# A residual attention and mixer layer on one core: another order of all operations, and the residual sums shared between VectorE and GpSimd

## The chip, the core and the metric

The kernel runs on one core of a Trainium2 chip. Its engines work side by side, each through its own list of instructions, and wait for each other by semaphores: TensorE (PE, matmuls; its weight loads are shown as PEld), VectorE (DVE), ScalarE (ACT), GpSimd (POOL) and SyncE (SP), which issues DMA transfers only. The metric is the device time of one execution in microseconds (us).

## The reference, cut to what matters

The input is one sequence of 2048 rows of 448 values in bf16. The layer normalises it, runs a sliding-window attention, adds the result to the input, and does the same once more with a mixer and MLP. The kernel must give `h2`.

```python
def _A_ref(x, wqkv, wo):                      # 16 heads of 28
    q, k, v = heads(x @ wqkv)
    idx = pos[:, None] - 2 * arange(8)[None, :]          # 8 keys, every second row back
    logits = einsum("bhsd,bhswd->bhsw", q, k[idx]) * 28 ** -0.5   # masked where idx < 0
    return merge(einsum("bhsw,bhswd->bhsd", softmax(logits), v[idx])) @ wo

def _B_ref(x, w1, w2, w3, w4):
    h = gelu(layernorm(x) @ w1)
    hs = shifted(h) @ w2          # four quarters of h, shifted by 1, -1, 2, -2 rows
    x1 = x + hs
    return x1 + gelu(layernorm(x1) @ w3) @ w4

h  = x + _A_ref(layernorm(x), A_wqkv, A_wo)
h2 = h + _B_ref(layernorm(h), B_w1, B_w2, B_w3, B_w4)
```

So the output is the sum of `h`, of `x1` (which holds a normalised `h`), and of the MLP's result.

## The kernel before, in words

**Tiles and phases.** The 2048 rows are 16 tiles of 128 rows, in four strips of four tiles. All of the sequence stays on the chip. For each strip the attention runs through these phases: N1 (statistics and normalising of x), A1 (projection to q and k, kept transposed), V (projection to v), A2 (products of q with the eight shifted k on VectorE, tile `qk_r`, which TensorE adds up per head), S (softmax: tiles `mx`, `ls`, `pb`), A3 (VectorE spreads the probabilities over a band with a mask, tile `bd_r` out of `bmask`, and TensorE multiplies the band with v, tile `vw`), O (projection by wo and addition of x). Then, per strip, B1 (layer norm, w1 and a gelu into the transposed hidden state). The second half runs over five units of tiles, 0-1, 2-5, 6-9, 10-13 and 14-15: B2 (w2 and the residual, `x1` in f32), T (layer norm of `x1`, a transposition), W3 (w3 and gelu, tile `h3T`) and B3 (w4 and the store, tile `ost`).

**Halos.** The attention looks 14 rows back, so a strip needs the end of the strip before it. Four small on-chip copies per strip bring it there, issued by SP; their sources are written by ScalarE's copies out of PSUM. In the order listings they are `arena<-arena` of 64x4x16, 64x3x16, 64x16 and 128x3x16.

**The residual sums.** After the layer norm of `x1` has read a tile, `phase_B2` adds `xin` (the tile `h`) to it: `xb[i] += xin[i]`, 128 x 448 in f32, once for each of 16 tiles (lines 919 and 920, shown as `arena<-arena,xin`). `store` (line 943) needs that sum, and the small product `mrs`, minus the mean times the reciprocal deviation, 128 x 4, which `rstd` (line 547) makes once per strip: it is the part of the normalised `h` that is the same for a whole row.

**What sets the order.** The program isn't emitted as it is written. Each operation is first recorded, with its engine and what it reads and writes (`_Sched.add` and `group`, lines 144 and 147); there are 858. `arrange` (line 194) then takes a table of numbers, `ORDER`: it is the sequence of all operations, and so the order on each engine, in SP's list of transfers, and the order in which the buffers of a pool are handed out (eight PSUM banks, three `lntm` of the layer norm, four `actT`, three `bd_r`, five `ost`, sixteen `h3T`). A second table, `OTHER`, names operations that take their alternative engine; until now only copies and normalises have one (ScalarE or VectorE, `copy`, line 403, and `normalize`, line 551). `_emit_plan` (line 247) sets the semaphores, and `emit_engine` (line 1002) writes the instructions, which is why all of them have line L1011 in the profile. `block` is an attribute of an operation that the recording keeps; nothing in `arrange` or `_emit_plan` reads it.

Of the kernel before, what the change touches and what calls it, by code (L numbers as in the profile page):

```python
# [6 lines left out]
ALU = mybir.AluOpType  # L7
# [12 lines left out]
STAGE = '....'  # L20
ALONE = False
ORDER = """
# [29 lines left out]
"""  # L52
OTHER = """
91 94 114 187 188 501 507 549 550
"""
FULL = (4,)
FILL = (1, 1, 0, 0)
# [228 lines left out]
def bass_sequential_preLN__sliding_local_dilated__mixer_s_mlp__prompt_kernel(  # L286
# [16 lines left out]
    S = _Sched()  # L303
# [16 lines left out]
    with ExitStack() as es:  # L320
        def sb(name, shape, dt):
            return es.enter_context(nc.sbuf_tensor(name, shape, dt))
        AR = sb("arena", [128, A_END], BF16)
        xin = sb("xin", [128, NTL, D], BF16)
# [17 lines left out]
        rs_y = sb("rs_y", [128, 3, 2, NTL], F32)  # L342
        mrs = sb("mrs", [128, NTL], F32)
        nm = sb("nm", [128, 3, NTL], F32)
# [21 lines left out]
        def arv(off, parts, n):  # L366
            return AR[0:parts, off:off + n]
# [12 lines left out]
        xb = [arv(A_KV + i // 4 * KVB, 128, 4 * D * 2).bitcast(F32).rearrange("p (i d) -> p i d", d=D)[:, i % 4, :] for i in range(NTL)]  # L380
# [18 lines left out]
        def act(out_ap, in_ap, func, **kw):  # L399
            table = {ACT.Exp: "exp", ACT.Ln: "exp", ACT.Gelu_apprx_tanh: "gelu"}.get(func)  # L400
            return S.add("act", "activation", table=table, out=out_ap, in_=in_ap, func=func, **kw)
# [7 lines left out]
        def dve(meth, block=False, **kw):  # L409
            op = S.add("dve", meth, **kw)  # L410
            op.block = block
            return op

        def pool(meth, **kw):
            return S.add("pool", meth, **kw)
# [90 lines left out]
        def rstd(kind, i, m=4, summed=False, norms="v", how="p"):  # L506
            var = mv[:, kind, i:i + m, 1]
            by = 1.0 / D if summed else 1.0
            first = int(kind == 1)
            shifted_ = "a" in norms  # L510

            def power(k):
                S.add("pool", "tensor_tensor", out=rs_y[:, kind, k, i:i + m], in0=rs_x[:, kind, k, i:i + m], in1=mhalf[:, 0:m], op=ALU.pow)

            def power_act(k):
                act(rs_x[:, kind, k, i:i + m], var, ACT.Ln, scale=by * (1.0 + EPS * k), bias=epsilon[:, k:k + 1])
                act(rs_y[:, kind, k, i:i + m], rs_x[:, kind, k, i:i + m], ACT.Exp, scale=-0.5)

            def shift(k):
                if m == 1:  # L520
                    act(nmr[:, kind, i:i + 1], nm[:, kind, i:i + 1], ACT.Identity, scale=rs_y[:, kind, k, i:i + 1])
                else:
                    dve("tensor_tensor", out=nmr[:, kind, i:i + m], in0=nm[:, kind, i:i + m], in1=rs_y[:, kind, k, i:i + m], op=ALU.mult)

            if not summed and (shifted_ or kind == 1):
                dve("tensor_scalar", out=nm[:, kind, i:i + m], in0=mv[:, kind, i:i + m, 0], scalar1=-1.0, scalar2=None, op0=ALU.mult)
            if how == "a":
                power_act(first)
                if shifted_:
                    shift(first)  # L530
                if kind == 1:
                    power_act(0)
            else:
                if kind == 1:
                    dve("tensor_scalar", out=rs_x[:, kind, 1, i:i + m], in0=var, scalar1=by * (1.0 + EPS), scalar2=EPS * EPS, op0=ALU.mult, op1=ALU.add)
                    power(1)
                    if shifted_:
                        shift(1)
                if kind == 1 or summed:
                    dve("tensor_scalar", out=rs_x[:, kind, 0, i:i + m], in0=var, scalar1=by, scalar2=EPS, op0=ALU.mult, op1=ALU.add)  # L540
                else:
                    dve("tensor_scalar", out=rs_x[:, kind, 0, i:i + m], in0=var, scalar1=EPS, scalar2=None, op0=ALU.add)
                power(0)
                if kind != 1 and shifted_:
                    shift(0)
            if kind == 1:
                pool("tensor_tensor", out=mrs[:, i:i + m], in0=nm[:, 1, i:i + m], in1=rs_y[:, 1, 0, i:i + m], op=ALU.mult)

        CHUNK = (0, 128, 192, 320)

# [337 lines left out]
        def phase_B2(u):  # L888
# [28 lines left out]
            for n, i in enumerate(tiles):  # L917
                normalize(2, i, ln, n, xb[i], TURN["B2"][u], summed, norms[n])
            for i in tiles:
                S.add("pool", "tensor_tensor", out=xb[i], in0=xb[i], in1=xin[:, i, :], op=ALU.add).block = True  # L920
            b2_a[u] = transposed(ln, TURN["B2"][u], len(tiles))

        h3 = {}
# [129 lines left out]
```

## Time and profile before

| what | value |
| --- | --- |
| time, median of 3 runs | 191.43 us (191.26 to 191.53) |
| profiled execution, its own time | 191.99 us |
| span of that execution in the trace | 190.3 us |
| PE busy | 180.0 us (95%), 2434 matmuls |
| DVE busy | 129.9 us (68%) |
| ACT busy | 123.4 us (65%) |
| POOL busy | 26.5 us (14%) |
| 16 residual sums on GpSimd | 17.1 us, 1086 ns each |
| granted TensorE clock | 1.00 |

In the rows of the profile an operation is named by engine, line, operation and `out<-in`, with buffer numbers left out; `xN` counts instructions that were put together. The bracket at a row's end is the idle time of the engine ahead of it and what ended that. A DMA row's time ends with its landing where the row says so, and SPq is the queue of SP's issues.

### The profile page before, as it was taken

To read this page: it belongs to the slowest core of one execution; us is meant where nothing else is said; L and a number is where in the kernel's file an instruction comes from. 1 tells how busy PE (TensorE), PEld (TensorE's weight loads), DVE (VectorE), ACT (ScalarE), POOL (GpSimd) and SP (SyncE) were. 2 spreads that over 40 slices of the span, in tenths; PEclk is the share of its full clock that TensorE was granted. 3 is DMA by queue.
4 is the path that set the end of the run, shared out by engine and by line. 5 is a ranking of instruction groups with operands and counts; after the bars stand their busy time and mean duration, and the time that the engine had idled before them with its cause. 6 is when DMAs were issued, how large, how long until landed. Compare 5 with 4: busy or idle time off the path is not lost.

```text
span 190.3 us, 5623 instructions
## 1 busy us (share of the span) xinstructions
PE 180.0 (95%) x2434; PEld 96.3 (51%) x2434; DVE 129.9 (68%) x226; ACT 123.4 (65%) x282; POOL 26.5 (14%) x61
## 2 busy tenths in 40 slices
PE   6699999897999989999989999999999999999994
PEld 2496433354443545565645535545444454455672
DVE  6999999999999999998998940099850006002203
ACT  3459999998999999999644897910256303650250
POOL 2250000000010000002205100181386002000000
DMA  5950254477407895796250060015044004000031
GB/s 147 339 193 3 44 110 110 78 174 158 103 3 114 160 272 225 136 331 134 50 113 0 5 134 0 3 30 108 0 91 119 0 0 112 19 3 0 17 109 48
DMA packets 36577, 18.06 MB, mean 95 GB/s; under 512 B 25304, under 2 KB 36040, under 8 KB 36552
## 3 DMA queue, kind: packets, MB, share of 16 engines
q1 hardware_dynamic: 36552, 17.70, 38.3%
q8 instruction: 19, 0.31, 0.7%
q14 instruction: 6, 0.05, 0.1%
HBM read 7.91 MB, written 1.84 MB: 51 GB/s over the span
## 4 chain that ended last, share of the span: by engine, by line
PE 56%; DVE 22%; ACT 11%; DMA 5%; SPq 2%; issue 2%; DVEq 0%; ACTq 0%
PE ps L1011 56%; DVE qk_r L1011 6%; DVE lntm L1011 5%; DVE bd_r L1011 4%; DMA arena<-in_A_wqkv_dram 3%; ACT lntm L1011 3%; SPq L1011 2%; DMA wo_s<-in_A_wo_dram 2%; ACT arena L1011 2%; DVE arena L1011 1%; ACT xin L1011 1%; DVE mx L1011 1%; DVE st L1011 1%; ACT h3T L1011 1%; ACT rs_x L1011 1%
## 5 line engine op out<-in xcount | busy, mean ns | idle before, releaser
L1011 PE MATMUL ps<-actT,arena 64*128 64x512 bf16 (+1 forms) x756 | 69.4, 329 | 0.9 <-ACT h3T L1011 0.4
L1011 ACT ACTIVATE h3T<-ps 128x512 bf16<-128x512 f32 (+1 forms) x70 | 30.8, 518 | 41.2 <-PE ps L1011 41.0
L1011 PEld LDWEIGHTS ps<-actT,arena 64*128 64x128 bf16 x756 | 37.3, 94 | 28.5 <-PE ps L1011 2.1
L1011 PE MATMUL ps<-arena,h3T 64*128 64x448 bf16 (+2 forms) x434 | 44.9, 343 | 0.4 <-DVE arena L1011 0.3
L1011 DVE SCALAR_TENSOR_TENSOR ost<-ps,mrs,arena 128x448 bf16<-128x448 f32 (+1 forms) x17 | 10.8, 650 | 40.6 <-PE ps L1011 40.6
L1011 ACT ACTIVATE arena<-ps 128x512 bf16<-128x512 f32 (+3 forms) x63 | 31.5, 541 | 3.7 <-PE ps L1011 3.2
L1011 PEld LDWEIGHTS ps<-arena,h3T 64*128 64x128 bf16 (+1 forms) x434 | 22.9, 94 | 20.0 <-DVE arena L1011 0.7
L1011 DVE TENSOR_TENSOR qk_r<-arena 128x4096 bf16<-128x4096 bf16 (+1 forms) x16 | 32.0, 2013 | 0.3 <-PE ps L1011 0.3
L1011 DVE TENSOR_TENSOR bd_r<-arena,bmask 80x2048 bf16<-80x2048 bf16 x16 | 19.8, 1270 | 0.1
L1011 POOL TENSOR_TENSOR arena<-arena,xin 128x448 f32<-128x448 f32 x16 | 17.1, 1086 | 14.8 <-DVE lntm L1011 14.8
L1011 DVE TENSOR_SCALAR lntm<-arena,mv,rs_y 128x512 bf16<-128x512 f32 x14 | 8.9, 679 | 12.2 <-ACT rs_y L1011 11.7
L1011 PE MATMUL ps<-wo_s,actT 64*128 64x448 bf16 x128 | 14.8, 350 | 1.1 <-DMA wo_s<-in_A_wo_dram 1.0
L1011 PE MATMUL ps<-w_s,arena 64*128 64x448 bf16 (+1 forms) x128 | 14.2, 350 | 0.1
L1011 PE MATMUL ps<-actT,w_s 64*112 64x512 bf16 x112 | 13.4, 378 | 0.0
L1011 ACT ACTIVATE actT<-ps 128x512 bf16<-128x512 f32 (+2 forms) x18 | 11.2, 653 | 3.2 <-PE ps L1011 3.2
L1011 PE MATMUL ps<-arena,actT 64*128 64x448 bf16 x112 | 13.2, 350 | 0.1
L1011 ACT ACTIVATE lntm<-xin,nm 128x448 bf16<-128x448 bf16 x16 | 10.5, 662 | 3.6 <-DVE nm L1011 3.6
L1011 POOL TENSOR_TENSOR mrs<-nm,rs_y 128x4 f32<-128x4 f32 x4 | 1.5, 387 | 71.9 <-ACT rs_y L1011 70.1
L1011 DVE SCALAR_TENSOR_TENSOR arena<-xin,rs_y,ps 128x448 f32<-128x448 bf16 x16 | 10.4, 667 | 0.0
L1011 DVE BATCH_NORM_STATS2 st<-xin 128x6 f32<-128x448 bf16 x16 | 9.2, 611 | 0.9 <-DMA xin<-in_A_x_dram 0.9
L1011 PEld LDWEIGHTS ps<-wo_s,actT 64*128 64x128 bf16 x128 | 5.6, 94 | 7.6 <-PE ps L1011 1.5
L1011 PEld LDWEIGHTS ps<-actT,w_s 64*112 64x112 bf16 x112 | 7.0, 127 | 4.7 <-DMA actT<-lntm 0.4
(70 smaller groups left out, 158.0 us busy)
## 6 DMA issues: line engine op xcount, KB each, us to landing
arena<-in_B_w_dram SPq DMA_DIRECT2D x2, 896.0 KB, 6.5
out_dram<-ost SPq DMA_DIRECT2D x15, 112.0 KB, 2.0
arena<-in_B_w_dram SPq DMA_DIRECT2D x2, 784.0 KB, 5.7
vw<-vt SPq DMA_DIRECT2D x4, 320.0 KB, 3.8
vw<-vt SPq DMA_DIRECT2D x4, 256.0 KB, 3.6
arena<-in_A_wqkv_dram SPq DMA_DIRECT2D x2, 448.0 KB, 4.7
xin<-in_A_x_dram SPq DMA_DIRECT2D x2, 448.0 KB, 7.2
xin<-in_A_x_dram SPq DMA_DIRECT2D x3, 224.0 KB, 5.9
```

The source lines that it names most:

```text
L1011: inst = getattr(eng, meth)(**kw)
```

## The change

Three things change.

1. `mrs` is made by VectorE instead of GpSimd: four products of 128 x 4.
2. A residual sum may be made by GpSimd or by VectorE. Operations 685, 686, 755, 756, 815, 816 and 551 take VectorE, so seven of the sixteen sums stand there and nine stay on GpSimd. The attribute `block` of the sums goes.
3. `ORDER` is another sequence of the same 858 operations. In `OTHER` the copies 91, 114, 501 and 507 and the normalise 188 leave, so ScalarE does them; the normalise 189 enters.

VectorE's operations go from 216 to 223, ScalarE's from 244 to 248, GpSimd's from 57 to 46; TensorE's 262 groups (2434 matmuls) and SP's 79 transfers are the same.

```diff
 ORDER = """
-29 0 6 7 1 2 30 31 8 48 49 50 51 9 53 54 52 11 10 60 61 58 59 32 55 56 57 62 63 64 65 39 40 41 42 43 44 45 46 47 87 89
...
+29 0 1 6 7 33 34 35 5 8 48 9 53 49 39 40 41 42 43 44 45 46 47 30 32 2 50 54 11 10 58 51 52 60 59 55 61 56 62 57 63 65
...
 OTHER = """
-91 94 114 187 188 501 507 549 550
+94 187 189 549 550 551 685 686 755 756 815 816
 """
...
             if kind == 1:
-                pool("tensor_tensor", out=mrs[:, i:i + m], in0=nm[:, 1, i:i + m], in1=rs_y[:, 1, 0, i:i + m], op=ALU.mult)
+                dve("tensor_tensor", out=mrs[:, i:i + m], in0=nm[:, 1, i:i + m], in1=rs_y[:, 1, 0, i:i + m], op=ALU.mult)
...
             for i in tiles:
-                S.add("pool", "tensor_tensor", out=xb[i], in0=xb[i], in1=xin[:, i, :], op=ALU.add).block = True
+                both = dict(out=xb[i], in0=xb[i], in1=xin[:, i, :], op=ALU.add)
+                S.add("pool", "tensor_tensor", alts=[("dve", [("tensor_tensor", both)])], **both)
```

The first place is VectorE at the end of the attention, where the last strip's softmax (`mx`, `pb`) and band products (`bd_r`) meet the first unit's layer norm (`st`, `mv`, `lntm<-arena`). Before:

```order
L1011 TENSOR_SCALAR rs_x<-mv 128x4
L1011 TENSOR_REDUCE mx<-ls 128x64
L1011 TENSOR_TENSOR pb<-ls,mx 128x8x64
L1011 TENSOR_SCALAR lntm<-arena,mv,rs_y 128x512 x2
L1011 TENSOR_SCALAR nm<-mv 128x4
L1011 TENSOR_SCALAR lntm<-arena,mv,rs_y 128x512
L1011 TENSOR_TENSOR bd_r<-arena,bmask 80x2048 x2
L1011 TENSOR_SCALAR lntm<-arena,mv,rs_y 128x512
L1011 TENSOR_TENSOR bd_r<-arena,bmask 80x2048
L1011 CAST actT<-ps 128x512
L1011 TENSOR_TENSOR bd_r<-arena,bmask 80x2048
L1011 CAST actT<-ps 128x512
```

and after:

```order
L1012 TENSOR_REDUCE mx<-ls 128x64
L1012 BN_STATS st<-arena 128x6
L1012 BN_AGGR mv<-st 128x2
L1012 TENSOR_TENSOR arena<-arena,xin 128x448
L1012 BN_STATS st<-arena 128x6
L1012 TENSOR_TENSOR mrs<-nm,rs_y 128x4
L1012 TENSOR_SCALAR nm<-mv 128x4
L1012 BN_AGGR mv<-st 128x2 x3
L1012 TENSOR_SCALAR rs_x<-mv 128x4
L1012 TENSOR_TENSOR pb<-ls,mx 128x8x64
L1012 TENSOR_SCALAR lntm<-arena,mv,rs_y 128x512
L1012 TENSOR_TENSOR bd_r<-arena,bmask 80x2048 x3
```

Behind these rows follow three normalises, the last product and then B3's eviction; the two casts are ScalarE's now, a residual sum and `mrs` have come in, and `pb` stands behind the statistics.

The second place is GpSimd from the end of the attention on, with `mrs`, the residual sums and the powers of the layer norm. Before:

```order
L1011 TENSOR_TENSOR rs_y<-rs_x,mhalf 128x4
L1011 MEMSET arena 128x4x2
L1011 TENSOR_TENSOR mrs<-nm,rs_y 128x4
L1011 TENSOR_TENSOR arena<-arena,xin 128x448
L1011 TENSOR_TENSOR mrs<-nm,rs_y 128x4
L1011 TENSOR_TENSOR arena<-arena,xin 128x448 x3
L1011 TENSOR_TENSOR mrs<-nm,rs_y 128x4
L1011 TENSOR_TENSOR arena<-arena,xin 128x448 x4
L1011 TENSOR_TENSOR rs_y<-rs_x,mhalf 128x2
L1011 TENSOR_TENSOR rs_y<-rs_x,mhalf 128x4
L1011 TENSOR_TENSOR arena<-arena,xin 128x448 x8
```

and after:

```order
L1012 TENSOR_TENSOR arena<-arena,xin 128x448
L1012 MEMSET mhalf 128x8
L1012 TENSOR_TENSOR rs_y<-rs_x,mhalf 128x4
L1012 TENSOR_TENSOR arena<-arena,xin 128x448
L1012 MEMSET arena 128x4x2
L1012 TENSOR_TENSOR arena<-arena,xin 128x448 x5
L1012 TENSOR_TENSOR rs_y<-rs_x,mhalf 128x4
L1012 TENSOR_TENSOR arena<-arena,xin 128x448 x2
L1012 TENSOR_TENSOR rs_y<-rs_x,mhalf 128x2
```

The products are gone, nine sums are left of sixteen, and most of them stand between the two powers.

The third place is SP's list after the loads of wqkv, with the halos of the first strips. Before:

```order
L1011 DMA xin<-in_A_x_dram 128x4x448 x2
L1011 DMA arena<-arena 128x3x16
L1011 DMA arena<-arena 64x4x16
L1011 DMA arena<-arena 64x3x16
L1011 DMA arena<-arena 64x16
L1011 DMA_TRANSPOSE actT<-lntm 128x16x128
L1011 DMA vw<-vt 16x3x512
L1011 DMA arena<-arena 64x3x16
```

and after:

```order
L1012 DMA xin<-in_A_x_dram 128x4x448
L1012 DMA arena<-arena 128x3x16
L1012 DMA xin<-in_A_x_dram 128x4x448
L1012 DMA vw<-vt 16x512
L1012 DMA arena<-arena 64x4x16 x2
L1012 DMA arena<-arena 64x16
L1012 DMA arena<-arena 64x3x16 x2
L1012 DMA_TRANSPOSE actT<-lntm 128x16x128
```

The 64x4x16 of the second strip and the 64x16 now stand ahead of the first 64x3x16. A little further on in the same list stood one load of wo, a 128x3x16 and three loads of wo; now there are two loads of wo, a 64x16, a load, a 64x3x16 and the last load.

56 rows, old and new, of the table ORDER are left out of this document.

## The prediction

> **What bounds the kernel now.** I read the chain of work that ended last first, because it says whose time counts where; then the busy time by stretches cut where the chain changes hands; then the timelines of the engines around each place where the chain leaves TensorE. These are four of the chain's 151 pieces, with start, length, engine and what it works on.
>
> ```profile
> 8.52 13.31 PE ps L1011 x209
> 39.90 4.17 DMA wo_s<-in_A_wo_dram
> 67.47 10.59 PE ps L1011 x164
> 127.75 59.27 PE ps L1011 x623
> ```
>
> The last piece is to be noted: from 127.75 us to 187.0 the chain is TensorE without a break. Ahead of it the chain changes hands often (VectorE, ScalarE, a load of wo), so an edit can win or lose time there, and from 127.75 on only if it makes TensorE wait. The stretches show the same. Columns are the stretch, its length, busy us and instructions of each engine, the granted clock, the share of the DMA engines, GB/s.
>
> ```profile
> core 0: us, PE busy (x) PEld busy (x) DVE busy (x) ACT busy (x) POOL busy (x), PEclk, DMA share, GB/s
> 8.50:97.30 88.80, 84.99 (x1435) 46.18 (x1435) 86.72 (x135) 80.53 (x192) 7.02 (x31) 1.00 0.55 133
> 97.30:127.75 30.45, 29.75 (x345) 15.39 (x346) 17.41 (x37) 19.99 (x39) 7.14 (x9) 1.00 0.20 40
> 127.75:187.70 59.95, 59.93 (x630) 32.34 (x630) 18.72 (x38) 19.38 (x42) 10.90 (x11) 1.00 0.20 49
> ```
>
> From 8.5 to 97.3 us VectorE is busy 86.72 of 88.80 us: every operation laid on it there shows, and TensorE, 84.99, has little room either. From 97.3 on VectorE has room (17.41 of 30.45, then 18.72 of 59.95) and TensorE lacks 0.70 and 0.02 us. That is all there is to win: 3.81 us of TensorE idle in the first stretch, 0.70 in the second. The granted clock is 1.00 everywhere, so no term comes from it. Below, ±0.2% (0.38 us) is about what a measurement of this kernel can tell from no change.
>
> **The change, part by part.** I count from the profiled run: its span of 190.3 us and 1.69 around it make 191.99, which is 0.56 above the median of 191.43. Differences are put on the median.
>
> *Head, to 8.5 us: 0.* The start of TensorE at 8.52 follows the load of wqkv, whose place ahead is kept. Bounds 0 to +0.3.
>
> *The attention stage: order on SP and ScalarE.* The new order puts small on-chip copies (the halos of k that the next strip needs) elsewhere among SP's transfers. These are SP's issues, the ScalarE copies that feed the halos, their first reader on VectorE, the median landing time of such a copy, and the place where TensorE waits for wo.
>
> ```profile
> 18.51 2.85 SPq L1011 DMA_DIRECT2D arena<-arena  x3
> ...
> 18.11 1.18 ACT L1011 ACTIVATE arena<-ps 64x256 bf16<-64x256 f32 x3
> ...
> 24.07 1.22 DVE L1011 TENSOR_TENSOR qk_r<-arena 128x2048 bf16<-128x2048 bf16 x1
> ...
> arena<-arena SPq DMA_DIRECT2D x4, 6.0 KB, 2.5
> ...
> 37.63 1.66 ACT L1011 ACTIVATE arena<-ps 64x256 bf16<-64x256 f32 x4
> ...
> 38.82 1.48 SPq L1011 DMA_DIRECT2D wo_s<-in_A_wo_dram  x3
> ...
> 44.11 0.93 PE L1011 MATMUL ps<-wo_s,actT 64*128 64x448 bf16 x8 [0.95 <-DMA wo_s<-in_A_wo_dram]
> ```
>
> The halo that the product at 24.07 reads (64x3x16) is the middle one of the three issued from 18.51 in 2.85 us, at about 0.95 each: issued by 20.1, landed by 22.6, and 1.5 us to spare. Afterwards two more halos stand ahead of it. At 0.65 each (half of 1.22 us for two, estimated between 1.48/3 and 0.95) it lands at 23.9; and if ScalarE's copies, which the new order puts behind others, come 1.4 us later, at 25.3. So VectorE waits between 0 and 1.2 us; I take 0.25, since the nearer case has everything in time. Behind a late halo in SP's queue stand the transposed load of the next strip and the vw copies, which VectorE and TensorE need only microseconds later.
>
> The second place: two halos of strip 2 now stand between the loads of wo. Their source is copied by ScalarE from 37.63 to 39.29, and SP waits in order, so the last piece of wo starts between 39.0 and 41.0 instead of 39.90 and lands 4.17 later at 43.2 to 45.2. TensorE now waits 0.95 for it at 44.11, so this is worth −0.9 to +1.1. I take +0.15, the middle with the lean that a waiting queue has. Last, a ScalarE activation of the layer norm ahead of a transposition's reader: +0.2 (0 to its own length of some 0.3). The stage: **+0.6**, from −0.9 to +2.5. The two copies and the normalise that go back to ScalarE here are held at 0, since ScalarE has 8.3 us free in 88.8; if that cover fails they are a rival, below.
>
> *83 to 99 us.* VectorE here takes a residual sum and the small product, and gives up a copy; the order also moves the products with bmask. Rows of GpSimd, VectorE and TensorE:
>
> ```profile
> 89.14 1.02 POOL L1011 TENSOR_TENSOR rs_y<-rs_x,mhalf 128x4 f32<-128x4 f32 x1 [32.22 <-DVE rs_x L1011]
> ...
> 92.40 1.03 POOL L1011 TENSOR_TENSOR arena<-arena,xin 128x448 f32<-128x448 f32 x1
> ...
> 56.19 0.73 POOL L1011 TENSOR_TENSOR mrs<-nm,rs_y 128x4 f32<-128x4 f32 x1 [43.70 <-ACT rs_y L1011]
> ...
> 102.09 0.20 POOL L1011 TENSOR_TENSOR mrs<-nm,rs_y 128x4 f32<-128x4 f32 x1 [8.66 <-ACT rs_y L1011]
> ...
> 90.26 0.69 DVE L1011 TENSOR_TENSOR pb<-ls,mx 128x512 bf16<-128x512 f32 x1 [0.61 <-ACT mx L1011]
> ...
> 92.40 2.11 DVE L1011 TENSOR_TENSOR bd_r<-arena,bmask 80x2048 bf16<-80x2048 bf16 x1
> ...
> 94.44 1.21 DVE L1011 TENSOR_TENSOR bd_r<-arena,bmask 80x2048 bf16<-80x2048 bf16 x1
> ...
> 97.16 0.68 DVE L1011 CAST actT<-ps 128x512 bf16<-128x512 f32 x1
> ...
> 97.30 0.42 PE L1011 MATMUL ps<-bd_r,vw 80*32 80x64 bf16 x32 [0.56 <-DVE bd_r L1011]
> ```
>
> A GpSimd sum of 1.03 us that starts together with a product makes that product 2.11 instead of 1.21 us: the two engines do not work side by side there, which costs VectorE 0.90. The other way round, the same small product on GpSimd takes 0.73 in one place and 0.20 in another.
>
> Costs on VectorE: one sum, by the nearest row (pb, two f32 inputs, 512 columns in 0.69) 0.69×448/512 = 0.60; the small product 0.15 (its size is that of a 128x4 operation, quoted in the next part at 0.16); and a wait of 1.05, because pb now stands behind the stats of the last tiles and the power on GpSimd (1.02 long) is needed by the normalises right behind it. Together 1.80. Gone from VectorE: the copy 0.68 (now ScalarE's), the wait of 0.61 ahead of pb, the 0.90 beside the sum. Together 2.19. Balance −0.39. TensorE waits 0.56 at 97.30 for the products, so up to 0.56 can be won; the last of the four products comes later in the new order, which can cost up to one product, 1.21. I take **−0.35**, nearly the balance, with −0.56 and +1.2 as ends.
>
> The Trainium skill, SBUF — State Buffer, section "SBUF: two separate sides", says that VectorE and GpSimd share one pair of ports as an exclusive lock, which goes for a whole instruction to whichever starts first, and that a VectorE operation with two SBUF inputs needs that pair against a GpSimd operation that reads SBUF. The rows at 92.40 agree with it. The rule speaks against the change: sums and pb on VectorE have two such inputs, and would hold up GpSimd's power and its nine remaining sums; with the lock the wait above is 1.05, without it 0.35, and the sum below would be −1.25 instead of −0.55.
>
> *104 to 111 us.* VectorE, GpSimd and TensorE rows, and a free instance of the same small VectorE operation.
>
> ```profile
> 104.34 0.94 DVE L1011 TENSOR_SCALAR nm<-mv 128x4 f32<-128x4 f32 x1
> ...
> 27.41 0.16 DVE L1011 TENSOR_SCALAR nm<-mv 128x4 f32<-128x4 f32 x1
> ...
> 102.24 3.02 POOL L1011 TENSOR_TENSOR arena<-arena,xin 128x448 f32<-128x448 f32 x3
> ...
> 106.14 4.51 PE L1011 MATMUL ps<-actT,arena 64*128 64x512 bf16 x40
> ...
> 111.05 4.82 PE L1011 MATMUL ps<-actT,arena 64*128 64x512 bf16 x42 [0.40 <-ACT h3T L1011]
> ```
>
> A 128x4 operation takes 0.94 us beside GpSimd's three sums and 0.16 alone. ScalarE's normalises and then gelus follow it, and TensorE waits 0.40 at 111.05 for the first gelus. In the new order the sums of these tiles come behind, so 0.78 on that path goes. More than the wait can't be won: 0.40 by its mark, 0.45 as I take it (the 40 matmuls ahead were spread over 4.91 where 42 take 4.82). **−0.45**, from −0.6 to 0.
>
> *118 to 128 us.* The normalises of the second unit, GpSimd's sums beside them, and TensorE.
>
> ```profile
> 123.34 1.08 DVE L1011 TENSOR_SCALAR lntm<-arena,mv,rs_y 128x512 bf16<-128x512 f32 x1 [11.71 <-ACT rs_y L1011]
> ...
> 125.52 0.54 DVE L1011 TENSOR_SCALAR lntm<-arena,mv,rs_y 128x512 bf16<-128x512 f32 x1
> ...
> 123.11 2.21 POOL L1011 TENSOR_TENSOR arena<-arena,xin 128x448 f32<-128x448 f32 x2
> ...
> 118.77 1.49 PE L1011 MATMUL ps<-arena,h3T 64*128 64x448 bf16 x14
> 120.09 3.19 PE L1011 MATMUL ps<-w_s,arena 64*128 64x448 bf16 x32
> ...
> 125.96 1.50 PE L1011 MATMUL ps<-arena,h3T 64*128 64x448 bf16 x14
> 127.75 2.44 PE L1011 MATMUL ps<-arena,h3T 64*128 64x448 bf16 x24 [0.29 <-DVE arena L1011]
> ```
>
> A normalise takes 1.08 us beside the sums and 0.54 alone. VectorE's eviction that TensorE waits for at 127.75 stands behind them. The 14 matmuls from 125.96 take 1.79 to the next group, those from 118.77 take 1.32: 0.47 lost. Afterwards no sum stands beside these normalises. **−0.45**, from −0.47 to 0.
>
> *128 us to the end.* Six sums on VectorE, 6×0.60 = 3.6 us on an engine with 41 us free here: 0. GpSimd's remaining chain of sums delays a store, whose cover is the other PSUM banks; the transposition for the fourth unit now stands behind three stores on SP, which lands about when TensorE wants it. I take **+0.1** for both, from 0 to +0.6.
>
> Sum: 0 + 0.6 − 0.35 − 0.45 − 0.45 + 0.1 = −0.55. So 191.43 − 0.55 = 190.9 us; the span, 190.3 − 0.55 = 189.75.
>
> **The rivals.** *SP's queue decides (slower).* If a halo that waits for ScalarE holds up what stands behind it at both places, the stage costs 1.2 + 1.1 + 0.2 = 2.5 instead of 0.6: 191.43 − 0.55 + 1.9 = 192.8; with one of the two at its end and the other half way, about 192.2. It decides (over +0.38) once the stage costs more than 0.6 + 0.55 + 0.38 = 1.53. For it: TensorE already waits 0.95 for wo. Against: the first halo had 1.5 us to spare.
>
> *ScalarE becomes the bound of the attention stage (slower).* Two copies go back to it there.
>
> ```profile
> L1011 ACT ACTIVATE actT<-ps 128x512 bf16<-128x512 f32 x14 | 8.0, 604 | 2.5 <-PE ps L1011 2.4
> ```
>
> At 0.604 each they cost 1.2 if nothing hides them: 192.1. Against: ScalarE's 80.53 of 88.80 busy us leave 8 us, but in the places where VectorE waits for its copies none.
>
> *A lock in a new place (same).* If one of GpSimd's sums falls on a product again, 0.90 comes back: 191.8 at most, less where TensorE has work. *Nothing comes of it (same):* TensorE is 95% busy and a wait that goes is followed by the next; 191.4. *The fourth unit's transposition is late:* +0.5 on the forecast, 191.4.
>
> *The attention stage is free.* The halos and wo land in time: −0.55 − 0.6 gives 190.3.
>
> **How the numbers follow.** Forecast 0.30 (its own range 190.4 to 191.2), stage free 0.12: faster 0.42. Lock 0.10, nothing 0.07, late transposition 0.03: same 0.20. SP's queue 0.22, ScalarE 0.16: slower 0.38. The range goes from the free stage with the later gains at their ends (190.3 − 0.2 − 0.2 − 0.2 = 189.7) to SP's queue at its end, 192.8, with 0.1 of the head: 192.9.
>
> **What would show it.** Right: no wait above 0.3 us at the product behind the first halo; TensorE's wait for wo not above 1.2; no small VectorE operation of 0.9 us around 104; TensorE's waits at 97, 111 and 127 gone or under 0.2; and the last stretch, from the first B3 after the second unit to the end, as long as before. Wrong: waits of over 1 us of VectorE or TensorE for halos or wo; ScalarE busy without a gap with VectorE waiting for it; or TensorE waiting in the last 60 us, where I have counted 0.1.

## The result, and the profile after

The changed kernel takes 189.81 us (median of 4 runs, 188.86 to 190.07) against 191.48 us of the kernel before (4 runs, 191.26 to 191.75): a ratio of 0.9906, 95% interval 0.9886 to 0.9926. On a second chip (first experiment) it came to 0.9947, 0.9929 to 0.9964. It is faster by 1.0 to 1.8 us, where 0.55 us had been forecast. The direction was right and the size was too small. Ratios are those of fast runs alone; one run below, 192.86 us at a granted clock of 0.991, was a slow one and is in its kernel's median but not in its ratio.

The profiled execution took 188.86 us with a span of 187.1, and is the fastest of its four: the others took 189.63 to 190.07. So the two traces differ by 3.2 us of span where the medians differ by 1.7; what the rest is comes below.

The chain of work that ended last, four pieces of it (start, length, engine, tile):

```profile
7.74 26.08 PE ps L1012 x349
66.35 7.96 PE ps L1012 x134
77.12 8.44 PE ps L1012 x128
88.82 95.76 PE ps L1012 x1110
```

From 88.82 us on it is TensorE without a break, where it was from 127.75 on before. The load of wo is no longer in it. Stretches of the changed kernel, in the columns shown ahead:

```profile
core 0: us, PE busy (x) PEld busy (x) DVE busy (x) ACT busy (x) POOL busy (x), PEclk, DMA share, GB/s
8.50:97.30 88.80, 86.39 (x1477) 45.69 (x1473) 86.70 (x137) 81.68 (x195) 6.25 (x24) 1.00 0.55 132
88.80:184.60 95.80, 95.75 (x1110) 52.77 (x1110) 43.15 (x92) 44.67 (x92) 13.08 (x12) 1.00 0.23 50
```

In the same 88.80 us TensorE now does 86.39 us of work instead of 84.99, with VectorE as full as before (86.70 and 86.72). From 88.8 on it lacks 0.05 us.

To see where the lead arises I put the two traces side by side by the work that TensorE had done (its 262 groups of matmuls are the same; each is counted at the shorter of its two spacings). The changed kernel is ahead by 0.4 us at 12 to 38 us, by 1.3 at 44, 1.0 to 1.1 from 55 to 92, 1.8 to 2.0 from 97 to 108, 2.7 at 114, 3.2 at 129, and 3.1 at the end. So the lead of this one trace has five places: the head (0.45), wo (0.9, of which 0.3 goes again), 97 (0.7 to 0.9), 111 (0.7) and 127 (0.5).

The rows of these places, of VectorE, GpSimd and TensorE after the change:

```profile
89.02 0.69 DVE L1012 TENSOR_TENSOR pb<-ls,mx 128x512 bf16<-128x512 f32 x1
90.63 0.55 DVE L1012 TENSOR_SCALAR lntm<-arena,mv,rs_y 128x512 bf16<-128x512 f32 x1 [0.92 <-POOL rs_y L1012]
91.28 3.49 DVE L1012 TENSOR_TENSOR bd_r<-arena,bmask 80x2048 bf16<-80x2048 bf16 x3
...
96.06 1.22 DVE L1012 TENSOR_TENSOR bd_r<-arena,bmask 80x2048 bf16<-80x2048 bf16 x1
...
102.31 0.17 DVE L1012 TENSOR_SCALAR nm<-mv 128x4 f32<-128x4 f32 x1
...
121.41 0.54 DVE L1012 TENSOR_SCALAR lntm<-arena,mv,rs_y 128x512 bf16<-128x512 f32 x1
```

```profile
89.22 1.37 POOL L1012 TENSOR_TENSOR rs_y<-rs_x,mhalf 128x4 f32<-128x4 f32 x1 [14.04 <-DVE rs_x L1012]
96.22 1.95 POOL L1012 TENSOR_TENSOR arena<-arena,xin 128x448 f32<-128x448 f32 x1 [5.63 <-DVE lntm L1012]
```

```profile
42.78 0.93 PE L1012 MATMUL ps<-wo_s,actT 64*128 64x448 bf16 x8
...
97.46 0.42 PE L1012 MATMUL ps<-bd_r,vw 80*32 80x64 bf16 x32
...
103.27 9.02 PE L1012 MATMUL ps<-actT,arena 64*128 64x512 bf16 x82
```

The four band products take 3.49 for three and 1.22: none is 2.11 any more. The small operation is 0.17 instead of 0.94, the normalises 0.54 instead of 1.08. Not every operation of VectorE had been held up: before the change, its evictions out of PSUM beside GpSimd's three sums took 0.62 to 0.67, and they take 0.62 to 0.68 now. Now GpSimd is the one that is held up: its power takes 1.37 instead of 1.02, the sum that starts at 96.22, behind the start of a product, 1.95 instead of 1.03. TensorE's marks of waiting at 44, 97, 111 and 127 are gone, and 82 matmuls run through where 40 and 42 had a gap of 0.40 between them.

### The profile page after: what moved, and what is told of

Same layout as the page of the kernel before. It is cut to its first block, busy times and chain, and to the rows that moved or that the text cites. A ratio compares the mean times of both kernels' runs of the same rounds, so it can differ in the third digit from the quotient of the medians.

```text
span 187.1 us, 5625 instructions
## 1 busy us (share of the span) xinstructions
PE 179.9 (96%) x2434; PEld 96.1 (51%) x2434; DVE 129.1 (69%) x233; ACT 124.6 (67%) x286; POOL 19.8 (11%) x50
## 4 chain that ended last, share of the span: by engine, by line
PE 78%; DVE 16%; ACT 3%; DMA 1%; issue 1%
PE ps L1012 78%; DVE bd_r L1012 7%; DVE qk_r L1012 4%; DVE lntm L1012 2%; DVE st L1012 1%; DMA xin<-in_A_x_dram 1%; DVE mx L1012 1%; DVE ls L1012 1%; ACT vt L1012 1%; ACT xin L1012 0%; ACT ls L1012 0%; DVE pb L1012 0%; ACT arena L1012 0%; ACT rs_x L1012 0%; ACT rs_y L1012 0%
## 5 line engine op out<-in xcount | busy, mean ns | idle before, releaser
L1012 PE MATMUL ps<-arena,h3T 64*128 64x448 bf16 (+2 forms) x434 | 45.4, 343 | 0.1
L1012 ACT ACTIVATE arena<-ps 128x512 bf16<-128x512 f32 (+3 forms) x64 | 32.3, 542 | 6.2 <-PE ps L1012 5.8
L1012 PEld LDWEIGHTS ps<-arena,h3T 64*128 64x128 bf16 (+1 forms) x434 | 23.6, 94 | 18.9 <-PE ps L1012 0.5
L1012 POOL TENSOR_TENSOR arena<-arena,xin 128x448 f32<-128x448 f32 x9 | 10.9, 1243 | 96.6 <-DVE lntm L1012 96.6
L1012 DVE TENSOR_TENSOR bd_r<-arena,bmask 80x2048 bf16<-80x2048 bf16 x16 | 18.8, 1215 | 0.2
L1012 DVE TENSOR_SCALAR lntm<-arena,mv,rs_y 128x512 bf16<-128x512 f32 x14 | 7.2, 537 | 13.2 <-ACT rs_y L1012 11.4
L1012 ACT ACTIVATE actT<-ps 128x512 bf16<-128x512 f32 (+2 forms) x21 | 12.8, 648 | 1.5 <-PE ps L1012 1.5
L1012 PEld LDWEIGHTS ps<-w_s,arena 64*128 64x128 bf16 (+1 forms) x128 | 6.0, 94 | 5.8 <-PE ps L1012 0.5
```

Source lines behind the costliest of these rows:

```text
L1012: inst = getattr(eng, meth)(**kw)
```

## The experiments

All are compared with the kernel before on the same chip. Theory A: the order makes the gain, above all that GpSimd's sums stand elsewhere. Theory B: the engine moves make it. A third, beside both: part of it is the luck of transfers.

**The changed kernel again.** Nothing is edited.

> The changed kernel once more, unaltered. In its first trace TensorE was 0.44 us ahead at 12 us, where the first pieces of x landed at 3.29 instead of 3.98 us. If that lead belongs to the new order, TensorE's main stream starts again by 7.8 us and the ratio stays near 0.990. If it was the luck of the first loads, the stream starts at 8.2 to 8.6 us, the span is 187.5 to 188.2 and TensorE's other waits stay as in the first trace.

190.28 us (7 runs, 188.79 to 190.88), ratio 0.9947 [0.9929, 0.9964]. Its trace is that of the first within 0.2 us at every point, span 187.1, and is again the fastest of its runs; the other six have spans of 188.0 to 188.8. TensorE's first projections start at 8.09 us. Over all traces of this study they start between 8.06 and 8.65 us where the head is the changed one and between 8.00 and 9.14 where it is the old one. So the 0.45 us of the head are mostly luck of the first loads. The piece of x that landed at 3.98 in the first trace of before lands at 3.33 to 3.41 in six of the seven later traces with the old head. The second piece of wqkv lands between 7.57 and 8.61 over all traces, and where it lands after 8.1 the projections start within 0.1 behind it, whatever the head.

**The engine moves undone.** The changed order, sums and products back on GpSimd.

```diff
 OTHER = """
-94 187 189 549 550 551 685 686 755 756 815 816
+94 187 189 549 550
...
-                dve("tensor_tensor", out=mrs[:, i:i + m], in0=nm[:, 1, i:i + m], in1=rs_y[:, 1, 0, i:i + m], op=ALU.mult)
+                pool("tensor_tensor", out=mrs[:, i:i + m], in0=nm[:, 1, i:i + m], in1=rs_y[:, 1, 0, i:i + m], op=ALU.mult)
```

> The new order, with all sixteen sums and the four small products back on GpSimd. If the order makes the gain, the time is within 0.4 us of the changed kernel (189.6 to 190.2), with longer small operations on VectorE where a sum stands beside them. If the engine moves make it, more than half of the gain goes: 190.7 us or more.

189.56 us, ratio 0.9920 [0.9897, 0.9943]: the whole gain is still there. Theory B falls for this order.

**The engine moves alone.** The order before, seven sums on VectorE.

```diff
 OTHER = """
-91 94 114 187 188 501 507 549 550
+91 94 114 187 188 501 507 549 550 551 685 686 755 756 815 816
```

> The order before, with the same seven sums on VectorE; the small products stay on GpSimd. If the order makes the gain: 191.2 to 191.7, no change that counts. If the engine moves make it: 190.7 or less, with normalises of 0.54 instead of 1.08 us around 123.

192.75 us, ratio 1.0085 [1.0063, 1.0107]: slower, which neither theory expected. Rows of VectorE, GpSimd and TensorE:

```profile
122.12 3.89 DVE L1012 TENSOR_SCALAR lntm<-arena,mv,rs_y 128x512 bf16<-128x512 f32 x4 [11.16 <-ACT rs_y L1012]
...
121.88 3.38 POOL L1012 TENSOR_TENSOR arena<-arena,xin 128x448 f32<-128x448 f32 x3
...
127.25 2.06 PE L1012 MATMUL ps<-arena,h3T 64*128 64x448 bf16 x20 [1.02 <-DVE arena L1012]
```

With some sums taken out of its list, GpSimd runs the next three one behind the other, and now all four normalises fall on them: 3.89 us for the four, where 0.54 each is free. TensorE waits 1.02 instead of 0.29. Later, at 159 and 181, TensorE waits about 0.25 each time for VectorE's evictions, which is new in this kernel too. The same kernel also shows the gain: only two sums follow each other at 101.71, the small operation at 103.81 takes 0.17, and TensorE gains 0.6 at 111. So what a sum costs goes by what stands beside it, and moving it to VectorE only changed which operations those are.

**One halo moved.** The order before, with the 128x3x16 halo that stood between the loads of wo moved up.

```diff
+DMA arena<-arena 128x3x16
 DMA_TRANSPOSE actT<-lntm 128x16x128
-DMA wo_s<-in_A_wo_dram 28x4x448
-DMA arena<-arena 128x3x16
-DMA wo_s<-in_A_wo_dram 28x4x448 x3
+DMA wo_s<-in_A_wo_dram 28x4x448 x4
```

> The order before, with one transfer moved: the 128x3x16 halo that stands between the loads of wo goes ahead of the transposition before them. If this halo's many small packets hold up wo, wo lands 0.7 to 1.2 us earlier, TensorE's wait of 0.95 at 44 goes, and the time is 190.5 to 191.1 (0.4 to 0.9 less). If what stands behind on VectorE takes the wait over, wo lands earlier and the time stays within 0.3 of 191.4. If the load of wo is limited by its own start, nothing moves.

191.16 us, ratio 0.9990 [0.9977, 1.0002]. TensorE's rows:

```profile
43.29 0.93 PE L1011 MATMUL ps<-wo_s,actT 64*128 64x448 bf16 x8
...
53.10 0.42 PE L1011 MATMUL ps<-bd_r,vw 80*32 80x64 bf16 x32 [0.34 <-DVE bd_r L1011]
```

The wait for wo is gone in the trace, as it is in the two further traces below that have this halo ahead; with the halo between the loads it is there in all five. So the halo did hold wo up. In three of those five the profile puts the wait down to ScalarE; but here the same matmuls start at 43.29, when the copy of ScalarE's that is named in one of them has only begun (43.28), so they do not need it. 10 us later TensorE waits 0.34 for VectorE, and 0.2 us of time is left, which the interval does not tell from nothing: here, where VectorE has no room, the removed wait is mostly paid again.

**The first halo.** The changed kernel, with the halo that had the least to spare put first.

```diff
-DMA arena<-arena 64x4x16 x2
+DMA arena<-arena 64x4x16
+DMA arena<-arena 64x3x16
+DMA arena<-arena 64x4x16
 DMA arena<-arena 64x16
-DMA arena<-arena 64x3x16 x2
+DMA arena<-arena 64x3x16
```

> The changed kernel with one halo moved in SP's list: the first 64x3x16, which landed only 0.2 us before VectorE needed it, goes ahead of two others. In both traces of the changed kernel the span was 187.1, in its other executions 187.7 to 188.8. If a late landing of this halo makes those longer, the median falls to 188.9 to 189.5, near the profiled 188.8. If something else does, the median stays at 189.8 to 190.3.

190.15 us, 188.99 to 190.57, ratio 0.9929 [0.9904, 0.9955]: not told apart from the changed kernel. The halo is not what spreads its runs. But this trace is of a longer execution (span 188.3), and shows what made this one longer: the second piece of wqkv landed at 8.49 instead of 7.59, and near 70 us the transposition for the second strip of the mixer landed at 70.70 instead of 68.44. TensorE is 0.46 behind the first trace of the changed kernel at 12 us and loses 0.75 more between 66 and 75, which together is the difference of the spans:

```profile
70.74 1.07 PE L1012 MATMUL ps<-actT,w_s 64*112 64x512 bf16 x8 [0.36 <-DMA actT<-lntm]
```

**Half and half.** Two kernels cut at about 84 us (after 484 of the 858 numbers): the first takes the order before up to there and the changed order after it, the second the reverse. Copies, sums and `mrs` stand on the engines of the half they come from.

```diff
 OTHER = """
-94 187 189 549 550 551 685 686 755 756 815 816
+91 94 114 187 188 549 550 551 685 686 755 756 815 816
...
 OTHER = """
-94 187 189 549 550 551 685 686 755 756 815 816
+94 187 189 501 507 549 550
```

> The order before up to about 84 us (the first 484 numbers), and from there the changed order, with its engine moves. By the traces the changed kernel gains 0.71 at 97, 0.72 at 111 and 0.48 at 127. If these places carry the gain: span shorter by 1.6 to 2.0 in the trace, time 189.5 to 190.1. If the gain comes from the head and the loads of wo: 191.0 or more.

> The changed order up to about 84 us, and from there the order before with its engines. If head and wo carry their part as in the traces (0.45 at the head, 0.9 at wo, 0.4 given back): 190.3 to 190.8. If they were luck of the loads: 191.2 to 191.7. If the attention stage costs what was forecast (+0.6): 192.

The late half alone: 189.93 us, ratio 0.9924 [0.9901, 0.9947]. The early half alone: 190.98 us, 0.9983 [0.9971, 0.9996]. So the late half brings 1.45 us and the early half 0.3. The two halves are not apart, though: the sum that stood beside the band product at 92 is at place 578 of the order before and at 451 of the changed order, so that both kernels run it at 74. Of the early half, GpSimd and VectorE:

```profile
74.12 1.26 POOL L1012 TENSOR_TENSOR arena<-arena,xin 128x448 f32<-128x448 f32 x1 [62.80 <-DVE lntm L1012]
...
92.25 2.35 DVE L1012 TENSOR_TENSOR bd_r<-arena,bmask 80x2048 bf16<-80x2048 bf16 x2
```

Two products take 2.35, where before they took 3.25, and TensorE gains 0.67 at 97 in this trace and 0.68 in that of the late half. The 0.3 of the early half is thus what is left of the gain at 97 after the attention stage has cost some 0.35 (a gain read from a trace, set against timed runs).

In the early half TensorE does not wait for wo but waits 0.64 further on, for ScalarE's copy behind the band products:

```profile
52.95 0.93 PE L1012 MATMUL ps<-wo_s,actT 64*128 64x448 bf16 x8 [0.64 <-ACT actT L1012]
```

**Four sums moved, nothing else.** The order before, and only GpSimd's list changed.

```diff
 TENSOR_TENSOR arena<-arena,xin 128x448
 TENSOR_TENSOR mrs<-nm,rs_y 128x4
-TENSOR_TENSOR arena<-arena,xin 128x448 x3
+TENSOR_TENSOR arena<-arena,xin 128x448
 TENSOR_TENSOR mrs<-nm,rs_y 128x4
-TENSOR_TENSOR arena<-arena,xin 128x448 x4
+TENSOR_TENSOR arena<-arena,xin 128x448 x6
```

> The order before, with four of GpSimd's sums moved behind the second unit's two, and nothing else: two no longer stand beside the small VectorE operation at 104, two no longer beside the normalises at 123. If the two engines block each other: that operation takes 0.16 instead of 0.94, the normalises 0.54 instead of 1.08 and 1.25, TensorE's waits at 111 and 127 go, and the time falls by 0.5 to 0.9, to 190.6 to 191.0. If the operations are short but other work takes the wait over: 191.3 or more.

190.15 us, ratio 0.9937 [0.9919, 0.9954], 1.2 us faster: more than the 0.5 to 0.9 expected, and no less than the whole change gave on the second chip (1.0). VectorE and TensorE:

```profile
103.51 0.17 DVE L1011 TENSOR_SCALAR nm<-mv 128x4 f32<-128x4 f32 x1
...
121.81 1.92 DVE L1011 TENSOR_SCALAR lntm<-arena,mv,rs_y 128x512 bf16<-128x512 f32 x4 [11.57 <-ACT rs_y L1011]
...
105.31 7.96 PE L1011 MATMUL ps<-actT,arena 64*128 64x512 bf16 x72
```

The four normalises take 1.92 us here, 3.89 beside GpSimd's sums in the experiment above. In its trace TensorE gains 0.72 at 111 and 0.47 at 127, together 1.2, which is the time.

**A fifth sum.** The one beside the band product at 92 goes ahead of the power.

```diff
+TENSOR_TENSOR arena<-arena,xin 128x448
 TENSOR_TENSOR rs_y<-rs_x,mhalf 128x4
 MEMSET arena 128x4x2
 TENSOR_TENSOR mrs<-nm,rs_y 128x4
-TENSOR_TENSOR arena<-arena,xin 128x448
```

> The kernel of the experiment on the four sums, with a fifth moved: the one that stood beside the band product at 92 goes ahead of the power, 15 us earlier. If the blocking there costs what the forecast's step took: the product takes 1.21 instead of 2.11, TensorE's wait of 0.5 at 97 goes, and the time falls by another 0.4 to 0.7, to 189.5 to 189.8. If VectorE has the room, or the sum falls on another operation at 75: 190.0 to 190.3.

189.66 us, ratio 0.9915 [0.9888, 0.9943]. The products run freely and TensorE's lead over the kernel with four sums moved grows by 0.62 at 97. The times alone would not tell the two kernels apart (0.9937 and 0.9915, intervals overlap); they agree with it. The trace is of the slowest of its ten executions (191.35 us, span 189.6; the others 187.5 to 188.4), and what it lost lies ahead of all this: the second piece of x landed at 4.03, TensorE's projections start at 9.14, and the first 84 of their matmuls take 5.67 us where they take 4.76 in the trace with four sums moved, at a granted clock of 1.00 in both. Why they were slow is open.

```profile
93.64 2.36 DVE L1011 TENSOR_TENSOR bd_r<-arena,bmask 80x2048 bf16<-80x2048 bf16 x2
```

**w2 earlier.** The changed kernel, one load moved ahead by some 13 us.

```diff
 DMA w_s<-in_B_w_dram 128x2x448 x2
+DMA w_s<-in_B_w_dram 112x4x448
 DMA_TRANSPOSE actT<-lntm 128x16x128
...
-DMA w_s<-in_B_w_dram 112x4x448
 DMA_TRANSPOSE actT<-lntm 128x16x128
```

> The changed kernel with one load moved in SP's list: w2, 224 KB and waiting for nothing, goes from right ahead of the first half's second transposition to right behind w1. In the traces of this order that transposition landed at 68.2 to 68.4 twice and at 70.2 to 70.7 three times, and in those TensorE lost about 0.7 near 70 us. If w2 in front of it makes it late: it lands by 68.5, TensorE waits less than 0.1 near 70, and the median falls by 0.3 to 0.8 below the changed kernel's, to 189.2 to 189.7. If the transposition is late by itself: 189.8 to 190.3.

189.22 us (189.10 to 189.83), ratio 0.9897 [0.9877, 0.9918]: the spread is down to 0.7 us, and the interval lies clear of that of the changed kernel's second comparison (0.9929 to 0.9964), though not of its first. The transposition landed at 67.27, the earliest of all traces.

**All of it by order.** The order before, with five sums, the halo and w2 moved, no engine changed.

```diff
+DMA arena<-arena 128x3x16
 DMA_TRANSPOSE actT<-lntm 128x16x128
...
 DMA w_s<-in_B_w_dram 128x2x448 x2
+DMA w_s<-in_B_w_dram 112x4x448
```

> The order before with the five sums moved on GpSimd, and two transfers moved in SP's list: the 128x3x16 halo ahead of the transposition, as tried alone, and w2 right behind w1. No engine move. If the effects add up (about 1.2 for four sums, 0.5 for the fifth, 0.2 for the halo, 0.3 for w2): 189.1 to 189.5, faster than the changed kernel. If they hide each other: 189.6 to 190.2.

189.35 us (189.09 to 189.65), ratio 0.9898 [0.9879, 0.9916]. Seven moved instructions in two lists give what the new order of 858 operations with its engine moves and w2 gives. Both kernels are as fast as or faster than the changed one.

**Engine moves undone beside w2**, with the edit of the second experiment, and three kernels with the four loads of wo put ahead of the transposition as well, in the two changed orders and in the one above:

```diff
+DMA wo_s<-in_A_wo_dram 28x4x448 x4
 DMA_TRANSPOSE actT<-lntm 128x16x128
-DMA wo_s<-in_A_wo_dram 28x4x448 x2
...
-DMA wo_s<-in_A_wo_dram 28x4x448
...
-DMA wo_s<-in_A_wo_dram 28x4x448
```

> The changed order with w2 moved, and all sixteen sums and the four small products back on GpSimd: what the engine moves are worth where the transposition near 70 us is no longer late. If they are worth nothing: within 0.3 us of the kernel with w2 moved, ratio 0.988 to 0.992. If VectorE's sums keep sums away from its own operations: some operations on VectorE are longer again, and the time is 0.4 us or more above it, 189.7 or more.

> The changed kernel with w2 early and the four loads of wo ahead of the transposition too, in the 4 us in which SP issues nothing. If wo's late landing in some executions is what is left of the spread: TensorE does not wait for wo, the times lie within 0.5 us of each other, median 188.7 to 189.2. If the transposition behind wo comes later instead and is waited for: 189.3 or more.

> The same with all sixteen sums and the small products back on GpSimd. If the engine moves are worth nothing beside the order: within 0.2 us of the one with them. If they are worth what the lower bound of the forecast's rows gives (one power's wait, 0.35 to 0.7): 0.3 to 0.7 us slower.

> The order before with the five sums moved on GpSimd, the halo and w2 moved, and wo early. If the new order has no gain beside sums, wo and w2: within 0.3 us of the changed kernel with wo and w2 early. If its attention stage is better or worse by itself: off by 0.4 or more.

With the engine moves undone: 189.76 us, 0.9911 [0.9881, 0.9941], against 0.9897 with them; its six runs again spread over 1.7 us (188.86 to 190.56), so w2 early does not remove the spread by itself. With wo early: the changed kernel 190.22 us, 0.9934 [0.9911, 0.9956]; without engine moves 189.35, 0.9891 [0.9862, 0.9920]; the old order with sums, halo, w2 and wo moved 189.24, 0.9906 [0.9875, 0.9936]. In the three pairs the kernel without engine moves is once slower by 0.14% and twice faster, by 0.27 and 0.43%: they are worth nothing that these runs can tell. Loading wo early brought nothing either. For the changed kernel the time fell in the range of the expectation's second case, but not for its reason: the transposition behind wo landed at 39.09, as early as in the first trace of the changed kernel within 0.15, and no wait for it is marked; TensorE stopped elsewhere, which the last section shows. The first of the four shows that wo can still be late, in the changed order too:

```profile
43.94 0.93 PE L1012 MATMUL ps<-wo_s,actT 64*128 64x448 bf16 x8 [1.05 <-DMA wo_s<-in_A_wo_dram]
```

## Why the prediction was too small, step by step

Two steps failed: within the attention stage the landing of wo got the wrong sign, and the gains behind the stage were held to TensorE's marked waits.

*The attention stage, +0.6: this step failed.* The landing of wo had been put at +0.15, between −0.9 and +1.1, "with the lean that a waiting queue has". The traces had the other answer: the old order also had a halo between the loads of wo, one of 384 packets of 32 bytes, and the new order takes that one out and puts smaller ones in. In five traces with the old list at wo TensorE waits 0.56 to 0.95 for it, in seven with the new list 0 to 0.2 in six and 1.05 in one. I had counted what the change puts into the queue and not what it takes out. The first halo, +0.25, cost nothing: it landed at 23.23, before the early end of the estimate of 23.9, and was needed at 23.43. That leaves a margin of 0.2 where there had been 1.95 (the prediction had read 1.5), and 0.05 to 0.37 in the other traces with this list. What the stage gives back (waits of 0.6 at 52.7 and up to 0.36 at 70) was not in the forecast as such; 0.2 had been set down for late transpositions.

What the whole stage cost is less sure than its terms. The early half's −0.3 (0.9983) holds 0.67 won at 97, which leaves +0.35. The whole change less the late half's −1.45 leaves −0.35 on the first comparison and +0.45 on the second, each known to about half a us. Between 12 and 92 us, against the first trace of before, TensorE gains −0.1 to 0.7 in five traces with the changed stage and w2 in its place, and 0.15 to 0.35 in four with the old one. So the best values lie between −0.35 and +0.45, all below the forecast, and where in between is open.

*83 to 99 us, −0.35: right cause, too small.* The wait for the power was 0.92 (forecast 1.05), the sum 0.59 (0.60), the small product 0.14 (0.15), the 0.90 beside the sum went. But the last product, for which I had held back part of the gain, made TensorE wait for nothing. 0.7 in the trace, 0.62 with the fifth sum alone.

*104 to 111 us, −0.45: right cause, too small.* 0.72, both in the changed kernel and where only four sums were moved. I had bounded the gain by TensorE's marked wait of 0.40. On VectorE 0.78 came free, and nearly all of it arrived: TensorE's matmuls ahead of the marked wait had been spread out as well, so that the mark shows only a part of the loss. For the same reason the 0.70 us of idle TensorE between 97.30 and 127.75 was not all that could be won there, as the prediction has it: 111 and 127 gave 1.2.

*118 to 128 us, −0.45:* 0.48. *128 us to the end, +0.1:* the lead falls by 0.09 there. Together these four had been put at −1.15; they are −1.8 in the trace, and the late half, which holds them all, measures −1.45. *Head, 0:* right, as the second run of the changed kernel showed; the 0.45 of the first pair of traces are mostly luck.

*The rule weighed ahead* (the Trainium skill, SBUF — State Buffer, "SBUF: two separate sides": the pair of ports goes to whichever starts first) agrees with the rows: with pb first, GpSimd's power took 1.37 us; with a product first, its sum 1.95; with GpSimd's sums first, VectorE's normalises took 3.89 for four. The normalises read one tile and two values per row, which the rule as the prediction tells it, for two inputs, does not clearly cover; the rows show the hold-up for them all the same. The rule gave the wait of 1.05, of which 0.92 came. That it speaks against the change was not borne out: the nine sums left on GpSimd now wait where nobody waits for them.

*The rivals.* SP's queue did not decide; ScalarE did not become the bound (81.68 of 88.80 us busy, against 80.53); "the attention stage is free", at 0.12, comes nearest, with later gains larger than their ends (0.7 at 97, 0.72 and 0.48 against 0.56, 0.6 and 0.47). The low end of the range, 189.7, took 0.2 off for each of the three gains, where those ends leave 0.21, 0.15 and 0.02, so 189.9: that 189.81 lies inside it owes to this and not to the working. The signs that the prediction named for being right all came: no wait at the product behind the first halo, none above 1.2 for wo, no small operation of 0.9 at 104, the waits at 97, 111 and 127 gone. They could not tell a gain of 0.55 from one of 1.7.

*What stays open.* Halves of 0.3 and 1.45 add up to 1.75, but count the gain at 97 twice; with it once they give 1.1, near the 1.0 of the second comparison and short of the 1.8 of the first. The changed kernel's timed runs, apart from the profiled ones, lie 0.8 to 2.1 us above its two traces; the landing of the transposition near 70 us (68.2 to 70.7 in traces of this order) and of wqkv and wo are seen to vary, but the timed runs have no trace, so their share is not shown.

## What to carry to other kernels

In this kernel GpSimd's sums should not stand beside VectorE's products and normalises on a path that is waited for. To find such places in another: look for operations of a known shape that are longer in one place than in another, and move the less urgent engine's work behind an operation that waits, since a place in a list alone does not delay it (the fifth sum, put ahead of the power, ran 15 us earlier). Count what an edit takes out of a transfer queue as carefully as what it puts in. And a wait that a trace marks can be less than what the late operation costs (0.40 marked at 111, 0.72 won), if the engine ahead of it was already being fed slowly.

## What the runs showed of the hardware

The traces have a queue of instructions, q8, that brings 19 pieces of 16,384 bytes in an execution and shares the DMA engines with the kernel's transfers. That these are TensorE's instructions is inferred from what follows, not shown. In 15 traces the piece that is fetched behind the transposition and ahead of most of w3 near 68 us came between 66.8 and 69.7 us, and TensorE went on. In the two others, both with wo early, it came at 70.0 and 70.6, in the midst of the loads of w3, and TensorE stopped in the middle of a group of 16 matmuls, with nothing that it waited for. The first of these, TensorE and then the DMA queues from 69.9 to 71.5 us (packets, MB, share of 16 engines):

```profile
72.39 0.74 PE L1012 MATMUL ps<-wo_s,actT 64*128 64x448 bf16 x5 [0.50 <-issue]
```

```profile
q1 hardware_dynamic: 189, 0.63, 98.8%
q8 instruction: 1, 0.02, 3.4%
```

The starts of two matmuls lie 0.85 us apart there, and 1.12 in the other trace. That the late piece is the cause is argued from this coincidence, not shown; a kernel that delays w3 could test it.
